# Batch 0's attention in pairs of chunks, W2 in contiguous rows, fewer filler matmuls, and a new order

## The chip, the core and the metric

The kernel runs on one core of one Trainium2 chip. The metric is the time of one execution on the device in microseconds (us). Three executions of the kernel before took 186.71, 187.40 and 190.95 us; the median, 187.4, stands for it. The engines are PE (matrix multiply; PEld is its loading of the stationary operand, which can run ahead), DVE and ACT (both read and write SBUF and the PSUM banks where matmuls put their results), POOL (SBUF alone), and SP, which here only issues DMAs. Each runs its own list of instructions in order and waits for the others at semaphores.

## The reference

Two parts in a row, for 4 batches, 8 heads of 48 columns (384 together) and 768 tokens. First a linear attention with a decaying state, for each batch and head:

```
for t in range(S):
    cur = einsum('bhd,bhe->bhde', u * k[t], v[t])
    y[t] = einsum('bhd,bhde->bhe', r[t], state + cur)
    state = w[t][..., None] * state + einsum('bhd,bhe->bhde', k[t], v[t])
```

Then, on x = y with the heads side by side (768 x 384 for each batch), a Fourier mix and a two-layer block:

```
mixed = real(fft(fft(x, axis=1), axis=2))
u  = x + mixed
un = (u - mean(u)) / sqrt(var(u) + 1e-6)
out = u + maximum(un @ w_ch1, 0) @ w_ch2      # 384 x 1536 and 1536 x 384
```

## The kernel before

**Attention.** `attention(b, c)` handles one chunk of 128 tokens, one token per partition, six chunks for each batch. It loads w, k, r and v of the chunk (`load_one`: for every token eight runs of 48 floats, 192 bytes), takes the logarithm of w on ACT, and sums it along the tokens by matmuls with triangular masks (L724, L728). Exponentials (L730, L743) turn the sums into factors; r and k are multiplied by them (L762, L519), transposed on PE (L778, L784) and copied out of PSUM (L542, L543). The scores (L794) are eight matmuls of 48 rows, for two heads side by side in the upper and the lower half of the array. They are masked on DVE (L799) and multiplied with v (L844); the state of the earlier chunks is added (L841). A chunk's own contribution to the state is summed on PE (L820, in batch 0 together with the old state through L817) and scaled on DVE (L828). The bonus term of u is computed without PE: r times k times u, summed over 48 columns (L751), times v (`vtd`, on POOL), added while y is taken from PSUM (L850).

**Mix and block.** `mix(b)` multiplies folded x by cosine and sine tables (L905 to L908), copies the result out and mirrors it (`hcs`, `hcr`), multiplies by the second set of tables (L931), adds x (`uf`, L933), takes mean and variance (L937, L939), transposes (L954, in batches 2 and 3 by a DMA) and runs the two layers in halves of 384 tokens: twelve groups of three matmuls with W1 (L978), a ReLU on ACT or DVE (L983, L985), then twelve matmuls with W2 for each 128 tokens (L996), and the output (L1000, DMA at L1004). The folding of x (`fold`, POOL or DVE) must have come for all six chunks before a batch's first mixing product is complete.

**Order.** All work is written as operations with numbers; `ORDER` names for every engine the sequence of these numbers, by hand of an earlier search, and the program waits only where an operation reads or overwrites what another engine makes. PSUM banks are given out in the same replay of the lists. SP issues all loads and outputs in the order of its list, POOL asks for the two weight matrices (`weights`, L702), each with a wait for one load of the inputs (`W_AFTER`). Input buffers are `NIN` = 7 for each of w, k, r and v.

**Filler.** While the tables of sines are made, PE runs 26 matmuls on a table (L1017), and `NW` = 32 more (L1053), whose results nobody reads, stand in its list among batch 0's attention.

Of the kernel before, what the change touches and what calls it, by code (L numbers as in the profile page):

```python
# [24 lines left out]
PAIR = 4  # L25
# [5 lines left out]
NW = 32  # L31
# [28 lines left out]
    "act": (  # L60
# [13 lines left out]
    "dve": (  # L74
# [323 lines left out]
def bass_rwkv6_finch__then__fnet_fourier_mix_kernel(  # L398
# [309 lines left out]
    def attention(b, c):  # L708
# [17 lines left out]
        if n >= 2:  # L726
            o.deps.add(masked[n - 2])
# [300 lines left out]
    for b in range(B):  # L1028
        if LATE_V and b == 0:
            for c in range(NC):  # L1030
                load(b, c)
# [55 lines left out]
```

## Time and profile before

| | |
|---|---|
| median of the three executions | 187.4 us |
| span of the profiled execution, first to last instruction | 184.6 us |
| PE busy | 175.4 us, 1718 matmuls |
| DVE, ACT, POOL busy | 154.4, 126.6, 103.6 us |
| moved by DMA | 28.99 MB in 116486 packets |
| first matmul with W1 (L978) | at 45.4 us |
| last matmul | ends near 182 us |

The profile comes from one execution, whose time lies beside the three above; its span leaves out what happens before the first and after the last instruction. Matmuls overlap in the array: one of 384 columns is shown with 326 ns, but the next starts 163 ns later, so busy time of PE is the union of such pieces. A line such as L519 is that of a helper through which many operations go; the names beside it (`rk`, `vtd`, `xf`) tell which one.

### The profile page before, as it was taken

The page shows a single profiled execution, that of the slowest core. Times are in us where ns is not written, and L with a number is a line of the kernel's source. Part 1 is how long each engine was busy: PE and PEld are TensorE (multiplying, and loading weights), DVE is VectorE, ACT ScalarE, POOL GpSimd, SP SyncE. Part 2 cuts the span into 40 slices and gives each one's busy share as a digit, 9 for nine tenths or more (in the row PEclk, how much of TensorE's full clock was granted, in tenths as well). Part 3 has the DMA queues.
Part 4 walks back from the last instruction along what each step waited for, and adds up shares of the span by engine and source line. Part 5 has one row for each costly group of instructions (what it writes and reads, how often), then busy time and mean ns, then how long its engine had stood idle before and what let it go on. Part 6 is the DMA issues. An engine that isn't in the chain of part 4 may idle for free.

```text
span 184.6 us, 4537 instructions
## 1 busy us (share of the span) xinstructions
PE 175.4 (95%) x1718; PEld 114.0 (62%) x1718; DVE 154.4 (84%) x360; ACT 126.6 (69%) x297; POOL 103.6 (56%) x125
## 2 busy tenths in 40 slices
PE   4988997988999999999999999999999999999994
PEld 2555654665566667767667766766666765665663
DVE  8779997999978999999998979999988878771134
ACT  4879696486885999798989897973852653125410
POOL 4038997775416967199899994999287100000000
DMA  6999998999999989999999997974780024330033
GB/s 122 205 203 196 183 208 159 196 187 187 184 190 188 201 168 242 204 219 209 186 250 185 212 216 117 220 140 107 170 181 0 4 85 97 74 109 22 0 128 128
DMA packets 116486, 28.99 MB, mean 157 GB/s; under 512 B 111345, under 2 KB 116082, under 8 KB 116466
## 3 DMA queue, kind: packets, MB, share of 16 engines
q1 hardware_dynamic: 114514, 26.36, 69.8%
q0 software_dynamic: 1952, 2.36, 7.7%
q8 instruction: 13, 0.21, 0.5%
q14 instruction: 7, 0.06, 0.1%
HBM read 23.59 MB, written 4.72 MB: 153 GB/s over the span
## 4 chain that ended last, share of the span: by engine, by line
PE 80%; POOL 7%; DVE 6%; DMA 2%; SPq 2%; issue 1%; ACT 1%; POOLq 0%; DVEq 0%; ACTq 0%
PE bank L996 26%; PE bank L978 26%; PE bank L931 6%; PE bank L908 3%; PE bank L1017 3%; PE bank L794 3%; DMA in_r<-in_r_dram 2%; SPq L563 2%; POOL rk L519 2%; PE bank L844 2%; PE bank L724 2%; PE bank L841 1%; PE bank L728 1%; POOL vtd L519 1%; PE bank L820 1%
## 5 line engine op out<-in xcount | busy, mean ns | idle before, releaser
L996 PE MATMUL bank<-w,ht 128*128 128x384 bf16 (+2 forms) x300 | 53.7, 320 | 0.0
L978 PE MATMUL bank<-unt,w 128*128 128x384 bf16 x288 | 53.3, 326 | 0.2 <-DVE unt L543 0.2
L985 ACT ACTIVATE ht<-bank 128x384 bf16<-128x384 f32 x78 | 35.6, 494 | 25.3 <-PE bank L978 25.0
L996 PEld LDWEIGHTS bank<-w,ht 128*128 128x128 bf16 x300 | 27.5, 98 | 15.8 <-issue 0.2
L978 PEld LDWEIGHTS bank<-unt,w 128*128 128x128 bf16 x288 | 26.8, 97 | 16.3 <-ACT unt L542 0.3
L799 DVE TENSOR_TENSOR ah<-bank,msk 128x512 bf16<-128x512 f32 x48 | 31.4, 680 | 3.3 <-PE bank L794 3.1
L519 POOL TENSOR_TENSOR vtd<-in_v,dc 128x384 f32<-128x384 f32 x24 | 20.7, 863 | 12.1 <-DVE dc L751 10.8
L519 POOL TENSOR_TENSOR rk<-rk,ub 128x384 f32<-128x384 f32 x22 | 22.9, 1042 | 6.9 <-DVE rk L519 6.7
L519 POOL TENSOR_TENSOR rkh<-in_k,e 128x384 bf16<-128x384 f32 x18 | 18.2, 1008 | 12.1 <-ACT e L743 12.0
L1000 DVE SCALAR_TENSOR_TENSOR osb<-bank,rstd,uf 128x384 f32<-128x384 f32 (+2 forms) x25 | 14.8, 594 | 11.8 <-PE bank L996 11.5
L519 POOL TENSOR_TENSOR rk<-in_r,in_k 128x384 f32<-128x384 f32 x18 | 18.0, 1000 | 4.3 <-DMA in_r<-in_r_dram 4.3
L542 ACT ACTIVATE rkt<-bank 128x512 bf16<-128x512 bf16 x29 | 16.9, 603 | 0.5 <-PE bank L778 0.2
L743 ACT ACTIVATE e<-bank 128x392 f32<-128x392 f32 (+1 forms) x24 | 11.7, 496 | 5.3 <-PE bank L737 3.0
L850 DVE TENSOR_TENSOR x<-bank,vtd 128x384 f32<-128x384 f32 x24 | 13.1, 551 | 2.3 <-PE bank L844 2.3
L730 ACT ACTIVATE bank<-bank 128x384 f32<-128x384 f32 x24 | 11.4, 479 | 4.4 <-PE bank L724 4.3
L533 ACT ACTIVATE un<-uf,agg 128x384 bf16<-128x384 f32 x18 | 10.6, 615 | 4.7 <-DVE agg L939 4.5
L933 DVE TENSOR_TENSOR uf<-bank,x 128x384 f32<-128x384 f32 x24 | 12.5, 546 | 1.4 <-PE bank L931 1.3
L762 DVE TENSOR_TENSOR rkh<-bank,in_r 128x384 bf16<-128x384 f32 x24 | 13.1, 548 | 0.7 <-ACT bank L730 0.6
L751 DVE TENSOR_REDUCE dc<-rk 128x8 f32<-128x384 f32 x24 | 12.9, 540 | 0.0
L937 DVE BATCH_NORM_STATS2 bst<-uf 128x6 f32<-128x384 f32 x24 | 12.7, 548 | 0.1
L533 ACT ACTIVATE vb<-in_v 128x384 bf16<-128x384 f32 x22 | 11.2, 520 | 1.8 <-DMA in_v<-in_v_dram 1.7
L533 ACT ACTIVATE lb<-in_w 128x384 bf16<-128x384 f32 x24 | 11.9, 520 | 0.6 <-DMA in_w<-in_w_dram 0.4
(128 smaller groups left out, 332.2 us busy)
## 6 DMA issues: line engine op xcount, KB each, us to landing
in_r<-in_r_dram SPq DMA_DIRECT2D x24, 192.0 KB, 3.9
in_k<-in_k_dram SPq DMA_DIRECT2D x24, 192.0 KB, 3.9
in_w<-in_w_dram SPq DMA_DIRECT2D x24, 192.0 KB, 3.9
in_v<-in_v_dram SPq DMA_DIRECT2D x24, 192.0 KB, 4.0
out_dram<-osb SPq DMA_DIRECT2D x23, 192.0 KB, 2.3
w<-in_moe_w_ch_dram POOLq DMA_DIRECT2D x2, 1152.0 KB, 13.4
out_dram<-osb SPq DMA_DIRECT2D x1, 128.0 KB, 1.8
rkt<-rkh SPq DMA_TRANSPOSE x6, 3.3
```

The costliest lines, as they stand in the source:

```text
L519: return lambda e: e.tensor_tensor(out=o, in0=a, in1=b, op=f)
L533: return lambda e: e.activation(o, a, f, **kw)
L542: {"act": lambda e: e.activation(o(), i(), ACTF.Copy), "dve": lambda e: e.tensor_copy(out=o(), in_=i())}, **kw)
L751: op("dve", v_1(DM), lambda e: e.tensor_reduce(out=dc[:, :], in_=rku[:, :, :], axis=mybir.AxisListType.X, op=ALU.add), r=[("RK", i2)], w=[ ...
L762: op("dve", v_1(DM), lambda e: e.tensor_tensor(out=rh[:, :, 0:D], in0=ps(tce)[:, 0:DM].rearrange("t (h d) -> t h d", d=D), in1=rt[:, :, :] ...
L799: masked[n] = op("dve", v_1(512), lambda e, x=x: e.tensor_tensor(out=ah[:, x:H:2, :], in0=ps(ta[x])[:, :].rearrange("p (h t) -> p h t", t= ...
L850: op("dve", v_1(DM), lambda e: e.tensor_tensor(out=xb[:, c, 0:DM], in0=ps(ty)[:, 0:DM], in1=vtd[:, :, :].rearrange("t h d -> t (h d)"), op ...
L937: op("dve", v_1(DM), lambda e, kb=kb, bs=bs: e.bn_stats(bs[:, :], uf[:, kb, :]), r=[("UF", i, kb)], w=[("BST", n % 4)])
L978: ins = e.matmul(ps(t)[:, 0:384], W1[:, m, 128 * j:128 * j + 128], unt[:, :, m, :], start=(m == 0), stop=(m == NM - 1))
L985: "act": lambda e, j=j, t=t, ht=ht: e.activation(ht[:, j, :], ps(t)[:, 0:384], ACTF.Relu, scale=-1.0)},
L996: ins = e.matmul(ps(t)[:, 0:hi - lo], ht[:, j, 128 * x:128 * x + 128], W2[:, j, lo:hi], start=(j == 0), stop=(j == NJ - 1))
L1000: op("dve", v_1(hi - lo) + 64, lambda e, kb=kb, t=t, o=o, lo=lo, hi=hi: e.scalar_tensor_tensor(out=o[:, lo:hi], in0=ps(t)[:, 0:hi - lo], s ...
```

## The change

Batch 0 is processed by a new function, `attention2`, in three pairs of chunks. A pair is loaded as 256 tokens, two neighbouring tokens on each partition: one DMA for each of w, k, r and v (`load_two`) with runs of 96 floats, 384 bytes. The even and the odd tokens (x = 0, 1) are kept as two operands of 128. The first chunk of the pair is then partitions 0 to 63, the second 64 to 127 (a = 0, 1):

- The cumulative sums need both operands: seven matmuls of 384 columns for a pair in place of four, with masks that stop at the half (`MSB`, `NLB`).
- The scores of a pair are 32 matmuls with 48 rows and 64 columns of output in place of 16 with 128; the masking instructions are as many and as large as before, with their own masks (`MSP`).
- The state and y sum over even and odd tokens, each matmul on 64 rows: twice as many of them. The bonus term, now kept in bf16, goes into y by two further matmuls with selection masks (`SEL`), so that the copy of y out of PSUM is a plain copy, on ACT or DVE.
- Transposed r is copied out with the even and odd tokens woven together again, so that its columns are in the order of the tokens.
- The masks are made in `halves`: an iota on POOL and twelve short operations on POOL and DVE at the start.

W2 is loaded with twelve contiguous rows on each partition instead of rows 128 apart; hidden unit 12p + j is then at partition p, so W1's columns for group j are taken 12 apart. `NW` falls from 32 to 8. The five lists of `ORDER` are new throughout. Batches 1 to 3 keep `attention`, and the scores, which went through a generator for an option that was off, are an operation of it. In the new POOL list eleven operations (three folds of batch 0 first) stand between the requests for W1 and for W2; in the old one W2 follows W1 directly. In the new SP list the last outputs are those of chunks 5 (in two pieces), 4 and 3 of batch 3; in the old one the two pieces of chunk 5 come last.

```diff
-PAIR = 4
+PAIRED = (0, 2, 4)
...
-NW = 32
+NW = 8
...
+    INA = {n: sb("in_%s" % n, [NIN, H * D], FP32) for n in "wkrv"}
+    INB = {n: [INA[n][:, i, :].rearrange("p (h d) -> p h d", d=D) for i in range(NIN)] for n in "wkrv"}
...
+    def load_two(c, n):
+        i = c % NIN
+        o = op("sp", 750, lambda e: e.dma_start(
+            INA[n][:, i:i + 2, :].rearrange("p x (h d) -> p (x h) d", h=H // 2),
+            src[n][0, :, c * CH:(c + 2) * CH, :].rearrange("h (t x) d -> t h (x d)", x=2)),
+               w=[("in", n, i), ("in", n, i + 1)], sem="in_%s%d" % (n, i), xfer=1423)
+        loads[0, c, n] = loads[0, c + 1, n] = o
...
+    def halves():
+        op("pool", 160, lambda e: e.iota(CJ[:, :], [[1, CH + 1]], base=-1, channel_multiplier=-2,
+                                         allow_small_or_imprecise_dtypes=True), w=["CJ"])
+        op("dve", 70, ts(TH[:, :], TC[:, 0:1], 63.5, -float(CH), ALU.is_gt, ALU.mult), r=["TC"], w=["TH"])
+        for i in range(2):
+            x = CJ[:, 1 - i:1 - i + CH]
+            either(140, 370, ts(MSP[i][:, :], x, TH[:, :], None, ALU.is_gt), r=["CJ", "TH"], w=[("MSP", i)])
+            either(140, 370, ts(SEL[i][:, :], x, TH[:, :], None, ALU.is_equal), r=["CJ", "TH"], w=[("SEL", i)])
...
-                          w=[n], sem=n, xfer=f)
+        for n, T, x, d, f in (("W1", W1, moe_w_ch1.rearrange("(q p) n -> p q n", p=128), 940, 8000),
+                              ("W2", W2, moe_w_ch2.rearrange("(p q) n -> p q n", p=128), 940, 7000)):
+            asked[n] = op("pool", d, lambda e, T=T, x=x: e.dma_start(T[:, :, :], x), w=[n], sem=n, xfer=f)
...
+    def attention2(c):
...
+        op("act", a_sb(2 * DM), act(L2[:, :, :, 0:D], wt, ACTF.Ln), r=win + ["LOGEXP"], w=lbs)
...
+        o = op("pe", mm(DM, 3), cums(t1, ((MSB[:, :], 0), (IDB[:, :], 0), (MSB[:, :], 1))), r=["MSB", "IDB"] + lbs, w=[t1])
+        op("pe", mm(DM, 2), cums(t0, ((MSB[:, :], 0), (MSB[:, :], 1))), r=["MSB"] + lbs, w=[t0])
+        op("pe", mm(DM, 2), cums(t2, ((NLB[:, :], 0), (NLB[:, :], 1))), r=["NLB"] + lbs, w=[t2])
...
+            def amat(e, x=x, ta=ta):
+                for q in range(HP):
+                    for a in range(2):
+                        for y in range(2):
+                            ins = e.matmul(ps(ta[y])[64 * a:64 * a + 64, 128 * q:128 * q + 128],
+                                           kT[x][64 * y:64 * y + D, q, 64 * a:64 * a + 64], rT[a][64 * y:64 * y + D, q, :])
+                return ins
+            op("pe", 450, amat, r=[("KTB", st4[x]), ("RTB", st4[0]), ("RTB", st4[1])], w=ta, tiled=True)
...
+                    for h in range(HP):
+                        for x in range(2):
+                            ins = e.matmul(ps(tds)[:, 96 * h:96 * h + 96], kflat[x][lo, 128 * h:128 * h + 128],
+                                           vb[x][lo, 2 * h:2 * h + 2, :].rearrange("t h d -> t (h d)"),
+                                           start=fst and x == 0, stop=(x == 1), skip_group_check=True)
...
+            def ymat(e, a=a, fst=fst, lo=lo, ty=ty, s_in=s_in):
+                for x in range(2):
+                    e.matmul(ps(ty)[:, 0:DM], SEL[x][lo, :], vtd[x][lo, :, :].rearrange("t h d -> t (h d)"), start=(x == 0), stop=False,
+                             skip_group_check=True)
+                for q in range(HP):
+                    if not fst:
+                        e.matmul(ps(ty)[:, 96 * q:96 * q + 96], rT[a][:, q, :], s_in[:, q, :], start=False, stop=False,
+                                 skip_group_check=True)
+                    for h in (2 * q, 2 * q + 1):
+                        for x in range(2):
+                            ins = e.matmul(ps(ty)[:, D * h:D * h + D], ah[x][lo, h, :], vb[x][lo, h, :], start=False, stop=(x == 1),
+                                           skip_group_check=True)
+                return ins
...
+            evict(lambda ca=ca: xb[:, ca, 0:DM], lambda ty=ty: ps(ty)[:, 0:DM], DM, r=[ty], w=[("X", 0, ca)])
+            fold(0, ca)
...
-                        ins = e.matmul(ps(t)[:, 0:384], W1[:, m, 128 * j:128 * j + 128], unt[:, :, m, :],
+                        ins = e.matmul(ps(t)[:, 0:384], W1[:, m, j:HID:NJ], unt[:, :, m, :],
...
-        step = 2 if b >= PAIR else 1
...
+        for c in range(NC):
+            if b == 0 and c in PAIRED:
+                attention2(c)
+            elif b or c - 1 not in PAIRED:
+                attention(b, c)
```

More of the change, by code (lines that the diff above doesn't have):

```diff
@@ L431, in bass_rwkv6_finch__then__fnet_fourier_mix_kernel @@
     NT = 4 if DMA_T < B * NC else 3
-    INB = {n: [sb("in_%s%d" % (n, i), [H, D], FP32) for i in range(NIN)] for n in "wkrv"}
+    INA = {n: sb("in_%s" % n, [NIN, H * D], FP32) for n in "wkrv"}
+    INB = {n: [INA[n][:, i, :].rearrange("p (h d) -> p h d", d=D) for i in range(NIN)] for n in "wkrv"}
     UB = sb("ub", [H, D], FP32)
-    LB = [sb("lb%d" % i, [H, 64], BF16) for i in range(NB)]
-    E2 = [sb("e2_%d" % i, [DM + H], FP32) for i in range(NB)]
+    LBA = sb("lb", [NB, H, 64], BF16)
+    LB = [LBA[:, i, :, :] for i in range(NB)]
+    E2 = [sb("e2_%d" % i, [DM + 2 * H], FP32) for i in range(NB)]
     RKH = [sb("rkh%d" % i, [2, H, 64], BF16) for i in range(NT)]
@@ L473, in bass_rwkv6_finch__then__fnet_fourier_mix_kernel @@
     ONE = sb("one", [2], BF16)
+    TH = sb("th", [1], FP32)
+    ONE4 = sb("one4", [2, 2], BF16)
+    CJ = SD[:, 0, 1, 0:CH + 1]
+    MSB, NLB, *MSP = (SD[:, 0, 0, 64 * i:64 * i + 64].bitcast(BF16) for i in range(6))
+    MSP, SEL = MSP[0:2], MSP[2:4]
+    HALVES = ["CJ", "MSB0", "NLB0", "MSB", "NLB"] + [(x, i) for x in ("MSP", "SEL") for i in range(2)]
     ONF = VTD[3].rearrange("p a b -> p (a b)")[:, 0:128]
@@ L551, in load @@
     def load(b, c):
+        if b == 0 and c in PAIRED:
+            for n in "wkrv":
+                load_two(c, n)
+                if c == 0 and n == "w":
+                    op("sp", 60, lambda e: e.dma_start(UR[0:1, :], u.rearrange("(o h) d -> o (h d)", o=1)), w=["UR"],
+                       sem="ur", xfer=300)
+                    bonus()
+            return
         for n in "wkr" + ("" if (b, c) in LATE_V else "v"):
@@ L585, in masks @@
         dset(384, ts(IDW[:, :], CI[:, :], 0.0, None, ALU.is_equal), r=["CI"], w=["IDB"])
+        if PAIRED:
+            halves()
         op("dve", 70, ts(PB[:, :, 0], TC[:, 0:1].to_broadcast([128, HP]), 63.5, -200.0, ALU.is_gt, ALU.mult),
@@ L589, in masks @@
            r=["TC"], w=["PB"])
+    def halves():
[6 more added lines that the diff above has]
+            either(140, 370, ts(SEL[i][:, :], x, TH[:, :], None, ALU.is_equal), r=["CJ", "TH"], w=[("SEL", i)])
+        either(140, 370, ts(MSB[:, :], CI[:, 128:256], 0.0, None, ALU.is_gt), r=["CI"], w=["MSB0"])
+        either(140, 370, ts(NLB[:, :], CI[:, 128:256], 0.0, -1.0, ALU.is_ge, ALU.mult), r=["CI"], w=["NLB0"])
+        either(50, 100, fill(MSB[0:64, 64:128], 0.0), r=["MSB0"], w=["MSB"])
+        either(50, 100, fill(NLB[0:64, 64:128], 0.0), r=["NLB0"], w=["NLB"])
+        either(50, 100, fill(ONE4[:, :, :], 0.0), w=["ONE4z"])
+        for a in range(2):
+            op("dve", 50, fill(ONE4[64 * a:64 * a + 64, a, :], 1.0), port=("dve",), r=["ONE4z"], w=[("ONE4", a)])
     def bonus():
@@ L700, in weights @@
     def weights():
-        for n, T, x, d, f in (("W1", W1, moe_w_ch1, 940, 8000), ("W2", W2, moe_w_ch2, 1070, 8000)):
-            asked[n] = op("pool", d, lambda e, T=T, x=x: e.dma_start(T[:, :, :], x.rearrange("(q p) n -> p q n", p=128)),
-                          w=[n], sem=n, xfer=f)
+        for n, T, x, d, f in (("W1", W1, moe_w_ch1.rearrange("(q p) n -> p q n", p=128), 940, 8000),
+                              ("W2", W2, moe_w_ch2.rearrange("(p q) n -> p q n", p=128), 940, 7000)):
+            asked[n] = op("pool", d, lambda e, T=T, x=x: e.dma_start(T[:, :, :], x), w=[n], sem=n, xfer=f)
@@ L874, in fold @@
         both = [("X", i, p), ("X", i, c)]
-        vec(DM, tt(sd[:, 0, 0:DM + 1], xb[:, p, 0:DM + 1], xb[:, c, 0:DM + 1], ALU.add), r=both, w=[("SD", z, 0)])
-        vec(DM, tt(sd[:, 1, 0:DM + 1], xb[:, p, 0:DM + 1], xb[:, c, 0:DM + 1], ALU.subtract), r=both, w=[("SD", z, 1)])
+        vec(DM, tt(sd[:, 0, 0:DM + 1], xb[:, p, 0:DM + 1], xb[:, c, 0:DM + 1], ALU.add), r=both, w=[("SD", z, 0)] + HALVES)
+        vec(DM, tt(sd[:, 1, 0:DM + 1], xb[:, p, 0:DM + 1], xb[:, c, 0:DM + 1], ALU.subtract), r=both, w=[("SD", z, 1)] + HALVES)
         have = [("SD", z, 0), ("SD", z, 1)]
@@ L1028, in bass_rwkv6_finch__then__fnet_fourier_mix_kernel @@
     for b in range(B):
-        if LATE_V and b == 0:
-            for c in range(NC):
-                load(b, c)
-        step = 2 if b >= PAIR else 1
-        for c in range(0, NC, step):
-            chunks = [attention(b, c + x) for x in range(step)]
-            parts = [next(x) for x in chunks]
-            def scores(e, parts=parts):
-                for f, _, _ in parts:
-                    ins = f(e)
-                return ins
-            op("pe", 207 * step, scores, r=sum([x[1] for x in parts], []), w=sum([x[2] for x in parts], []), tiled=True)
-            for x in chunks:
-                next(x, None)
-            if b * NC + c + 1 == LOG_FIRST:
-                sines()
-                mirrors()
-                tables_end()
+        for c in range(NC):
+            if b == 0 and c in PAIRED:
+                attention2(c)
+            elif b or c - 1 not in PAIRED:
+                attention(b, c)
         if b == 0:
```

117 lines of the change are left out of this document (115 added, 2 removed), and 122 rows, old and new, of the table ORDER.

## The prediction

> **What bounds the kernel now.** I read the stretches of the span first, cut where the matmul engine changes its kind of work: up to 8.7 us tables and early filler, to 45.4 us batch 0's attention and its mixing, then W1 and W2 matmuls of all batches with the later attention between, to 182.1 us. Columns: stretch, length, then busy time and instructions of PE, weight loads, DVE, ACT, POOL, then granted clock, DMA share and GB/s.
>
> ```profile
> 8.70:45.40 36.70, 32.63 (x393) 20.77 (x393) 32.99 (x74) 28.34 (x61) 27.48 (x32) 1.00 1.01 191
> 45.40:182.10 136.70, 136.58 (x1300) 90.10 (x1300) 113.76 (x243) 92.68 (x227) 74.25 (x79) 1.00 0.72 148
> ```
>
> The second stretch is a PE bound: 136.58 of 136.7 us busy. The first (the **front**) is not: PE is idle for 4.1 us, and part of its busy time is filler. The same view for the filler's line alone (columns end with clock, DMA and rate), and the chain of waits for what one matmul costs in a stream (start, length, engine, line, count):
>
> ```profile
> 8.70:45.40 36.70, 7.52 (x32) 2.66 (x32) 1.00 1.01 191
> ```
> ```profile
> 86.03 0.22 PE bank L784 x4
> 86.25 0.20 PE bank L844 x8
> 86.45 2.93 PE bank L978 x18
> ...
> 42.62 0.17 PE bank L820 x4
> ...
> 42.95 0.33 PE bank L794 x8
> ```
>
> A 384-column matmul takes 2.93/18 = 0.163 us of PE, a transpose 0.055, a 48-column one 0.025, a 96-column one 0.043, one of the scores (L794) 0.041. So the 32 fillers hold PE for 5.2 us, and the front's other 361 matmuls, each at its slot, for about 23 us: 51 of 384 or 386 columns 8.3, 38 of half that 3.1, 77 transposes 4.2, 56 scores 2.3, 48 of 96 columns 2.0, 48 of 48 columns 1.2, 40 small sums 1.0, the bonus broadcast 0.9. PE has 36.7 - 28 = 8 to 9 us to spare there, half of it hidden in the modelled ends of matmuls.
>
> What holds the front? The timeline about 31 us (bracket: idle before, and what ended it):
>
> ```profile
> 30.48 0.52 ACT L533 ACTIVATE vb<-in_v 128x384 bf16<-128x384 f32 x1 [1.31 <-DMA in_v<-in_v_dram]
> 30.60 0.83 POOL L519 TENSOR_TENSOR vtd<-in_v,dc 128x384 f32<-128x384 f32 x1 [1.06 <-DMA in_v<-in_v_dram]
> ...
> 31.55 0.40 PE L794 MATMUL bank<-rkt 48*128 48x128 bf16 x8 [1.12 <-ACT rkt L542]
> ...
> 31.99 0.69 DVE L799 TENSOR_TENSOR ah<-bank,msk 128x512 bf16<-128x512 f32 x1 [1.38 <-PE bank L794]
> ```
>
> All four engines stand because the values of chunk 4 land at 30.5 us; the DMA engines are full (1.01). But DVE is busy 33.0 of 36.7 us, so only about 1.4 us is lost there. The end of the front is a chain through DVE to the first W1 matmul; the weights come as late:
>
> ```profile
> 44.91 0.36 DVE L543 COPY unt<-bank 128x384 bf16<-128x384 bf16 x1
> ...
> 45.41 1.30 PE L978 MATMUL bank<-unt,w 128*128 128x384 bf16 x7 [0.15 <-DVE unt L543]
> ```
> ```profile
> 34.35 0.93 POOL L702 DMA_DIRECT2D w<-in_moe_w_ch_dram  x1
> 36.59 1.06 POOL L702 DMA_DIRECT2D w<-in_moe_w_ch_dram  x1 [1.31 <-DMA in_r<-in_r_dram]
> ```
> ```profile
> DMA to landing us min/median/max: 10.5/13.4/16.2
> ```
> ```profile
> 53.22 0.65 PE L996 MATMUL bank<-w,ht 128*128 128x384 bf16 x3
> ```
>
> W1 lands at 34.35 + 10.5 = 44.9, half a microsecond before it is read (the 16.2 would be too late for 45.41, so it is W2's); W2 at 36.6 + 16.2 = 52.8, 0.4 us before its first matmul.
>
> ```profile
> span 184.6 us, 4537 instructions
> ```
> ```profile
> 182.10 0.35 DVE L1000 SCALAR_TENSOR_TENSOR osb<-bank,rstd,uf 128x128 f32<-128x128 f32 x1 [0.19 <-PE bank L996]
> ```
>
> The profiled execution's span is 184.6 us, of which 2.5 follow the last matmul; 2.8 us lie around the span to the median of 187.4, and I count on the same 2.8 after.
>
> **The change part by part.** The end is (first W1 matmul) + (PE work left) + (tail), so I price each term.
>
> *Loads.* One packet's time comes from the DMA view of 5 to 15 us (only 192-byte runs) and that of 170 to 184.6 us (nearly only 1536-byte rows): packets, MB, share of 16 engines.
>
> ```profile
> q1 hardware_dynamic: 10809, 2.05, 105.0%
> ```
> ```profile
> q1 hardware_dynamic: 1008, 1.18, 23.4%
> ```
>
> That is 1.05 x 160/10809 = 15.5 ns at 190 bytes (16 engines for 10 us) and 0.234 x 233.6/1008 = 54 ns at 1170, so 0.039 ns a byte and 23 ns at 384. A load of two chunks has 1024 such packets, 64 for each DMA engine: 1.5 us, where two loads take 2.0 (ends: 1.0, if a packet costs the same; 2.0, if only bytes count). Twelve of them: 17.7 us for 23.8. In the new SP order v of chunks 4 and 5 is the 13th load of data: some 19 us of transfers with it, so it is in by 23 us and not at 30.5. The wait goes; what is late next is arithmetic. W2 in rows of 12 has one run per partition; at best it costs what W1's bytes cost, about 1 us of DMA less, used in the next term.
>
> *Extra matmuls*, three pairs: cumulative sums 9 x 0.163 = 1.5; the bonus now enters y through two selection matmuls, 12 x 0.163 = 2.0; y in halves 48 x 0.025 = 1.2; state in halves 20 x 0.043 = 0.9; scores in quarter tiles, 96 for 48. The last has no row: if four run abreast it costs nothing more, one after another as transposes do 96 x 0.055 - 2.0 = 3.3; I take L794's 0.041: 2.0. Sum 7.5 us (5.5 to 8.9). Removed: 24 fillers, 3.9. [...] No row here has a column tile.
>
> *DVE, ACT, POOL.* The y add leaves DVE (L850) for a plain eviction, five of six on ACT:
>
> ```profile
> L850 DVE TENSOR_TENSOR x<-bank,vtd 128x384 f32<-128x384 f32 x24 | 13.1, 551 | 2.3 <-PE bank L844 2.3
> L542 ACT ACTIVATE st<-bank 128x384 bf16<-128x384 f32 x12 | 5.8, 486 | 0.0
> ```
>
> DVE loses 5 x 0.55 = 2.7 us, ACT gains 5 x 0.49 = 2.4 and has 8.4 idle. In the front DVE takes back about 2 us of batch 1's instructions that the new order puts ahead (two masks of 0.68, one r product, one copy). Nine of the 13 mask operations go to DVE beside the table work of the first 9 us; they hide behind the early filler, which ends at 8.7, and cost up to 1 us if they don't. With the 1.4 us stall gone DVE alone could bring W1 to 45.4 - 2.1 = 43.3.
>
> POOL before it asks for W1 does 5 k products, 6 r products, 6 vtd and 5 folds instead of 3, 7, 6 and 8, and two masks: as long, without the 1.06 us wait, but its second k product now waits for the second pair's exponentials. Its prices:
>
> ```profile
> L519 POOL TENSOR_TENSOR rk<-in_r,in_k 128x384 f32<-128x384 f32 x18 | 18.0, 1000 | 4.3 <-DMA in_r<-in_r_dram 4.3
> ...
> L519 POOL TENSOR_TENSOR xf<-x 128x192 bf16<-128x192 f32 x5 | 2.9, 594 | 0.0
> ```
>
> I put the request at 33.6 (from 32.5 to 35) and W1 at 33.6 + 10.5 = 44.1. Behind W1 three folds, two products, a vtd, two k products, two fills and a product stand ahead of W2 on POOL, 1.8 + 2 + 0.8 + 2 + 0.4 + 1 = 8 us where 1.3 us of wait stood: W2 is asked for at 42.5, and with W1's 10.5 lands at 53.0. The vtd among them waits for a DVE reduction ordered just before the first mixing result, so a late DVE is passed on to W2 and by it to PE, in order, behind the first L996.
>
> *PE's own bound.* 23.1 + 7.5 + 8 fillers 1.3 + 1.6 of batch 1's matmuls that move ahead of W1 (scores 0.33, y 0.2, two sums 0.33, two totals 0.3, eight transposes 0.44) is 33.5: without any gap W1 starts at 42.2; with the 4.2 us of gaps now hidden in busy time, at 46.4. I take **44.0**, between these, with POOL's 44.1 and DVE's 43.3 about it. Then the first W2 matmul, 8.9 us on in the new order (12 groups of 0.49, the rest attention), is at 52.9, with W2 just landed.
>
> *Sum.* PE work after the first W1 matmul: 136.7 - 1.6 = 135.1. End of PE 44.0 + 135.1 = 179.1. The tail grows: the last output was the split one, now it is a whole chunk.
>
> ```profile
> L1000 DVE SCALAR_TENSOR_TENSOR osb<-bank,rstd,uf 128x384 f32<-128x384 f32 x23 | 13.9, 609 | 11.3 <-PE bank L996 11.1
> ...
> L1000 DVE SCALAR_TENSOR_TENSOR osb<-bank,rstd,uf 128x128 f32<-128x128 f32 x1 | 0.4, 351 | 0.2 <-PE bank L996 0.2
> ```
> ```profile
> out_dram<-osb SPq DMA_DIRECT2D x5, 192.0 KB, 1.9
> ...
> out_dram<-osb SPq DMA_DIRECT2D x1, 64.0 KB, 1.6
> ```
>
> That adds 0.26 + 0.3, with a queue of two outputs close together 0.7: 2.5 becomes 3.2 us. Span 182.3, with 2.8 around it **185.1 us**, 2.3 less than the median.
>
> **W1 by stride.** With W2 in contiguous rows, W1's columns are taken 12 apart, 24 bytes, in all 288 weight loads of L978. Nothing in this trace strides a weight load. What contiguous ones cost, four against one:
>
> ```profile
> 31.88 0.10 PEld L734 LDWEIGHTS bank<-pb,idw 128*128 128x128 bf16 x1
> 31.89 0.18 PEld L737 LDWEIGHTS bank<-one,lb 128*128 128x128 bf16 x4
> ```
>
> (0.18 - 0.10)/3 = 27 ns apart, so a load has a sixfold margin under the 163 ns of the matmul that it hides behind. Ends: no cost; twelvefold by bytes stepped over, 324 ns and (324 - 163) x 288 = 46 us. I take none, being nearest to the only row. [...]
>
> **The rivals.**
> 1. *The front shrinks further* (chance 0.28). Scores four abreast and fewer gaps: extras 5.5, W1 near 42, W2 asked for earlier by as much. 185.1 - 2.5 = 182.6 (181 to 183.6). For it: PE idles 4.1 us now behind one late load. Against: DVE and POOL come out at 43.3 and 44.1.
> 2. *The gain is eaten* (0.20): PE's gaps stay as they are (W1 at 46.4), or W2, which now has eight microseconds of POOL work ahead of it, lands two or three microseconds after it is wanted. 185.1 + 2.4 = 187.5 (186.6 to 190). For it: W2's 16.2 us before, and every engine of the front near full.
> 3. *Slower: strided weight loads* (0.14). Place: L978, in the stretch that is PE's alone. Every nanosecond over 163 is paid 288 times, 0.29 us; at 190 ns, seven times the contiguous load and well short of the twelvefold end, 7.8 us: 193. It decides from 163 + 2300/288 = 171 ns on, six times the contiguous load. Against: a margin of six.
> 4. *The loads gain nothing* (0.04): at 2.0 us a pair the late v comes at about 29 us and the extra matmuls are pure cost: 185.1 + 4 = 189.
>
> **How the numbers follow.** Forecast 185.1, chance 0.34, own range 183.7 to 186.6. Two per cent (3.7 us) is about what a measurement of this kernel can tell: the three runs lie between 186.7 and 191.0. Faster than 183.7: rival 1 and a little of the forecast, 0.30. Slower than 191.1: rival 3 and the ends of 2 and 4, 0.18. Between them 0.52. Leaving out rival 3 and the lowest end, the range is 181.3 to 190.5.
>
> **What would show it.** Loads right: transfers of batch 0 over by 23 us and no engine waiting for a DMA near 30. Front right: first L978 at 43 to 45, less than 2 us of PE idle before it. W2: an idle PE ahead of the first L996 says rival 2. Strides: a run of L978 at 163 ns a matmul says none; 170 and more, rival 3. Extras: the PE line for the quarter scores at 0.3 to 0.7 us for 16. The tail: 3.2 us after the last matmul. I would be wrong above all if one late engine in the front holds the three others, since their orders are fixed.

## The result and the profile after

The changed kernel takes 199.0 us (median of four runs, 198.5 to 200.7), 1.065 times the kernel before (95% interval 1.056 to 1.073): 6.5% slower, where 185.1 us, 2.3 less than before, were forecast. Ratios, here and below, leave out executions more than 1.5% above the fastest of their kernel; the kernel before has such ones too, most of them at 195 to 200 us with a mean clock of 0.965 to 0.982. The page of the changed kernel gives the span and, in 40 slices of it, the clock that PE was granted:

```profile
span 197.2 us, 4772 instructions
...
PEclk9999955555999999999999999999999999999999
```

Five slices of the front ran at half clock. The view of stretches, cut where the clock changes and at the first W1 matmul (columns as in the prediction: stretch, length, busy time and instructions of PE, weight loads, DVE, ACT and POOL, then clock, DMA share, GB/s):

```profile
8.70:24.90 16.20, 14.72 (x223) 9.29 (x221) 13.96 (x35) 13.38 (x28) 12.18 (x16) 1.00 1.05 253
24.90:48.70 23.80, 23.80 (x212) 14.78 (x212) 12.74 (x25) 11.95 (x26) 12.51 (x18) 0.50 0.96 182
48.70:58.60 9.90, 9.85 (x119) 6.88 (x118) 8.44 (x21) 8.40 (x18) 6.68 (x10) 1.00 0.26 33
58.60:194.00 135.40, 134.24 (x1267) 100.67 (x1263) 116.51 (x248) 87.43 (x214) 69.63 (x75) 1.00 0.62 132
```

For 23.8 us PE was busy at 0.50. At full clock that work would take about 14 us. This is an estimate: the 16 groups of y in it (shown below) take 0.47 us each and 0.35 at full clock, and the rest is halved, as matmuls of 386 columns are (0.32 us apart from 46.14 us on, 0.16 from 49.08 on). So the low clock costs some 10 us. DVE, ACT and POOL were busy for only half of that stretch: they waited for PE, directly or through one another (between 8.7 and 58.6 us ACT waited 4.3 us and DVE 3.3 for matmuls of L889, and POOL 6.2 for ACT's copies of y). From the first W1 matmul on nothing is lost: 135.4 us to the end of PE's work, where the prediction had 135.1. The whole miss lies ahead of the first W1 matmul.

What PE did as the clock fell and as it came back, in the timeline of the changed kernel (start, length, engine, line, tiles, stationary rows and columns, shape, count):

```profile
21.81 0.42 PE L844 MATMUL bank<-rkt 48*64 48x128 bf16 x16 [0.41 <-DVE ah L849]
22.16 0.49 PE L881 MATMUL bank<-vtd,sd 64*128 64x384 bf16 x2
22.59 0.22 PE L885 MATMUL bank<-st,rkt 128*128 128x96 bf16 x1
22.74 0.27 PE L889 MATMUL bank<-vb,ah 64*128 64x48 bf16 x4
22.94 0.22 PE L885 MATMUL bank<-st,rkt 128*128 128x96 bf16 x1
...
44.31 0.26 PE L885 MATMUL bank<-st,rkt 128*128 128x96 bf16 x1
44.51 0.34 PE L889 MATMUL bank<-vb,ah 64*128 64x48 bf16 x4
44.78 0.61 PE L975 MATMUL bank<-idw,rkh 128*128 128x128 bf16 x4
...
48.83 0.24 PE L1097 MATMUL bank<-cn,xf 128*128 128x193 bf16 x1
```

Each y of a pair's half, the first of all apart, changes four times from matmuls on 64 rows (L881, L889) to one on 128 rows (L885) and back. A group of one L885 and four L889 takes 22.94 - 22.59 = 0.35 us at full clock and 44.78 - 44.31 = 0.47 at half; in the kernel before, one full-row state matmul and two full-row ones take 0.093 by the prediction's slots (0.043 + 2 x 0.025). The clock fell 2.7 us after the first such y began, while the longest idle of PE here is 0.41 us, and it came back 4 us after the last of them had ended (44.78 to 48.8).

Other rows that answer to those of before. First W1 matmul; POOL's requests for W1 and W2, and their landing; the last outputs:

```profile
58.61 1.17 PE L1169 MATMUL bank<-unt,w 128*128 128x384 bf16 x6
```
```profile
41.22 1.00 POOL L741 DMA_DIRECT2D w<-in_moe_w_ch_dram  x1
...
56.98 0.61 POOL L741 DMA_DIRECT2D w<-in_moe_w_ch_dram  x1
```
```profile
DMA to landing us min/median/max: 9.0/9.2/9.4
```
```profile
193.52 1.27 DVE L1191 SCALAR_TENSOR_TENSOR osb<-bank,rstd,uf 128x384 f32<-128x384 f32 x2 [0.30 <-PE bank L1187]
```

### The profile page after: what moved, and what is told of

It reads as the page before. It is cut to its first block, busy times and chain, and to the rows that moved or that the text cites. A ratio compares the mean times of both kernels' runs of the same rounds, so it can differ in the third digit from the quotient of the medians.

```text
span 197.2 us, 4772 instructions
## 1 busy us (share of the span) xinstructions
PE 189.6 (96%) x1836; PEld 134.9 (68%) x1836; DVE 159.9 (81%) x372; ACT 127.1 (64%) x293; POOL 102.7 (52%) x127
## 4 chain that ended last, share of the span: by engine, by line
PE 78%; SPq 6%; DVE 6%; DMA 5%; ACT 2%; issue 1%; POOL 1%; DVEq 0%; POOLq 0%; ACTq 0%
PE bank L1169 21%; PE bank L1187 19%; SPq L583 6%; PE bank L1122 5%; PE bank L1099 4%; PE bank L1208 4%; PE bank L889 3%; DMA in_w<-in_w_dram 3%; PE bank L985 2%; DMA in_k<-in_k_dram 2%; PE bank L885 2%; PE bank L881 2%; PE bank L915 1%; PE bank L919 1%; PE bank L1035 1%; DVE ah L849 1%
## 5 line engine op out<-in xcount | busy, mean ns | idle before, releaser
L1176 ACT ACTIVATE ht<-bank 128x384 bf16<-128x384 f32 x69 | 32.2, 501 | 20.6 <-PE bank L1169 20.3
L1169 PEld LDWEIGHTS bank<-unt,w 128*128 128x128 bf16 x288 | 39.4, 144 | 6.0 <-issue 0.2
L523 POOL TENSOR_TENSOR vtd<-in_v,dc 128x384 f32<-128x384 f32 (+1 forms) x23 | 19.1, 835 | 12.4 <-DVE dc L942 9.9
L990 DVE TENSOR_TENSOR ah<-bank,msk 128x512 bf16<-128x512 f32 x36 | 22.8, 680 | 1.8 <-PE bank L985 1.7
L523 POOL TENSOR_TENSOR rk<-rk,ub 128x384 f32<-128x384 f32 x19 | 19.1, 1013 | 2.9 <-DVE rk L523 2.7
L537 ACT ACTIVATE un<-uf,agg 128x384 bf16<-128x384 f32 x21 | 12.7, 632 | 8.1 <-DVE agg L1130 8.1
L1174 DVE TENSOR_SCALAR ht<-bank 128x384 bf16<-128x384 f32 x27 | 14.0, 551 | 4.2 <-PE bank L1169 4.2
L523 POOL TENSOR_TENSOR xf<-sd 128x384 bf16<-128x384 f32 (+1 forms) x12 | 12.4, 1041 | 9.4 <-DVE sd L523 9.4
L1124 DVE TENSOR_TENSOR uf<-bank,x 128x384 f32<-128x384 f32 x24 | 12.7, 547 | 1.1 <-PE bank L1122 1.0
L537 ACT ACTIVATE lb<-in_w 128x384 bf16<-128x384 f32 (+1 forms) x21 | 11.8, 566 | 2.8 <-DMA in_w<-in_w_dram 1.5
L953 DVE TENSOR_TENSOR rkh<-bank,in_r 128x384 bf16<-128x384 f32 x18 | 9.9, 550 | 2.9 <-ACT bank L921 1.8
L1041 DVE TENSOR_TENSOR x<-bank,vtd 128x384 f32<-128x384 f32 x18 | 9.9, 548 | 0.5 <-PE bank L1035 0.3
## 6 DMA issues: line engine op xcount, KB each, us to landing
out_dram<-osb SPq DMA_DIRECT2D x23, 192.0 KB, 2.2
in_w<-in_w_dram SPq DMA_DIRECT2D x18, 192.0 KB, 4.0
in_r<-in_r_dram SPq DMA_DIRECT2D x18, 192.0 KB, 4.1
in_v<-in_v_dram SPq DMA_DIRECT2D x18, 192.0 KB, 4.0
in_k<-in_k_dram SPq DMA_DIRECT2D x18, 192.0 KB, 3.8
```

The costliest lines, as they stand in the source:

```text
L523: return lambda e: e.tensor_tensor(out=o, in0=a, in1=b, op=f)
L537: return lambda e: e.activation(o, a, f, **kw)
L990: masked[n] = op("dve", v_1(512), lambda e, x=x: e.tensor_tensor(out=ah[:, x:H:2, :], in0=ps(ta[x])[:, :].rearrange("p (h t) -> p h t", t= ...
L1124: op("dve", v_1(DM), lambda e, kb=kb, t=t: e.tensor_tensor(out=uf[:, kb, :], in0=ps(t)[:, 0:DM], in1=xb[:, kb, 0:DM], op=ALU.add), r=[t, ( ...
L1169: ins = e.matmul(ps(t)[:, 0:384], W1[:, m, j:HID:NJ], unt[:, :, m, :], start=(m == 0), stop=(m == NM - 1))
L1174: {"dve": lambda e, j=j, t=t, ht=ht: e.tensor_scalar(out=ht[:, j, :], in0=ps(t)[:, 0:384], scalar1=-1.0, scalar2=0.0, op0=ALU.mult, op1=AL ...
```

## The experiments

Three theories stood at first. **C**: the 24 removed fillers let the clock fall. **S**: the strided weight loads cost the time. **P**: the pairs' row and column tiled matmuls pull the clock down, whatever stands between them.

### Fillers back in the changed kernel

```
-NW = 8
+NW = 32
 # 24 more in PE's order: ahead of scores, transposes, y and state of 16 to 30 us
```

> The changed kernel with 24 more warming matmuls in batch 0's attention, 32 in all as before the change. Theory C (the removed warming matmuls let the granted clock fall to half from 25 to 47.5 us, 22.5 us at half speed, some 11 us lost): granted clock 1.00 throughout, first W1 matmul at 47 to 49 us instead of 58.7, span 185 to 188, time 188 to 191, within 2% of the kernel before. Theory S (the strided weight loads cost the time): no change, 198 to 200. Theory P (the row and column tiled matmuls of the pairs pull the clock down whatever stands between them): clock again at 0.50 for some 20 us, 198 to 201.

Measured: 196.1 us (median of six), ratio 1.052 (1.048 to 1.055). The profiled execution, the shortest with 193.0 us, had clock 1.00 all through; the others had a mean clock of 0.965 to 0.982. So with 32 fillers the clock held in one execution of six and fell less in the other five than in the changed kernel (0.939 to 0.948); but even with the clock full the first W1 matmul was late:

```profile
22.28 0.50 PE L883 MATMUL bank<-vtd,sd 64*128 64x384 bf16 x2
22.71 0.22 PE L887 MATMUL bank<-st,rkt 128*128 128x96 bf16 x1
22.86 0.27 PE L891 MATMUL bank<-vb,ah 64*128 64x48 bf16 x4
23.06 0.22 PE L887 MATMUL bank<-st,rkt 128*128 128x96 bf16 x1
...
52.59 1.17 PE L1171 MATMUL bank<-unt,w 128*128 128x384 bf16 x6
```

That is the timeline of this run: again 0.35 us for a group (22.71 to 23.06), and W1 at 52.6, not at 47 to 49. PE had become the bound of the front: it was busy for all of the seven stretches of 2 us from 18 to 32 us (2.00 in each). Theory C explains the clock at best in part, and none of the rest. Theory P's 20 us at half, whatever the fillers, didn't come either: 0.965 is about 14 us (2 x 0.035 x 197), an estimate that takes the whole shortfall as time at half; for the changed kernel's 0.939 it gives 24.1, where 23.8 were measured.

### Fillers out of the kernel before

```
-NW = 32
+NW = 8
 # indices 1446 to 1469 struck from PE's order, nothing else
```

> The kernel before with its last 24 warming matmuls taken out (8 left), all else as it was. Theory C: the granted clock falls to half somewhere between 15 and 35 us, time 193 to 200. Theory P and theory S: clock stays 1.00, time 186 to 190, or a little less than before, since 3.9 us of matmuls are gone.

Measured: 186.3 us, ratio 0.996 (0.992 to 1.000). One dip of the clock, in the view of stretches of this run:

```profile
8.70:20.50 11.80, 9.81 (x110) 5.83 (x107) 9.83 (x22) 9.65 (x22) 6.84 (x7) 1.00 0.98 192
20.50:24.20 3.70, 3.46 (x42) 3.08 (x42) 3.34 (x8) 2.36 (x6) 3.70 (x6) 0.56 1.05 208
24.20:45.20 21.00, 17.87 (x226) 11.55 (x222) 20.58 (x46) 16.04 (x35) 18.83 (x23) 1.00 1.08 198
```

It lasted under 4 us and cost nothing: the first W1 matmul came at 45.25, against 45.41. Theory C falls: taking the fillers away is not enough to lose the time, since in this kernel the clock is back at 24.2 us with the 24 gone. It can still be needed beside something else.

### The old loads of W1 and W2 in the changed kernel, and the new ones in the kernel before

```
-("W2", W2, moe_w_ch2.rearrange("(p q) n -> p q n", p=128), 940, 7000)
+("W2", W2, moe_w_ch2.rearrange("(q p) n -> p q n", p=128), 940, 7000)
-W1[:, m, j:HID:NJ]
+W1[:, m, 128 * j:128 * j + 128]
```

and the reverse of it in the kernel before.

> The changed kernel with W2 again loaded in 12 separated rows per partition and W1's columns again taken as 128 neighbours: the weight loads of the W1 line are contiguous. Theory C: weight loads fall from 144 to about 97 ns on the profile's line, but the time stays at 197 to 200, since the W1 matmuls stream at the same spacing as before. Theory S: 193 or less (at least 20 ns on each of 288 loads, 6 us).

> The kernel before with only W2 loaded in contiguous rows and W1's columns taken 12 apart. Theory C: 186 to 190, no difference, clock 1.00, W1 matmuls 0.163 us apart in a stream. Theory S: 193 or more, spacing 180 ns and over.

Measured: the changed kernel with the old loads 197.3 us, ratio 1.056 (1.051 to 1.062), with a half-clock stretch again (0.65 from 24 to 26 us and 0.50 from 26 to 32, mean clock 0.937 to 0.945 in the four executions); the kernel before with the new loads 187.2 us, ratio 1.004 (1.000 to 1.008). The line of W1's matmuls and its weight loads (nanoseconds min/median/max), in the changed kernel and, below, with the old loads:

```profile
L1169 PEld LDWEIGHTS bank<-unt,w x288: 138/143/168, 58.6 to 188.6; 128*128 128x128 bf16 x144
L1169 PE MATMUL bank<-unt,w x288: 323/326/383, 58.6 to 188.7; 128*128 128x384 bf16 x144
```
```profile
L1169 PEld LDWEIGHTS bank<-unt,w x288: 95/98/99, 58.4 to 187.1; 128*128 128x128 bf16 x144
L1169 PE MATMUL bank<-unt,w x288: 322/326/337, 58.5 to 187.3; 128*128 128x384 bf16 x144
```

A strided weight load is 45 ns longer in the middle and still lies beside its matmul, whose median stays at 326 ns. Only a few are late (383 against 337 at most); over the 245 spacings of neighbours in the trace, what lies above 163 ns adds up to 0.5 us (0.03 with the old loads). Theory S falls: that half microsecond comes after the first W1 matmul, and is no part of the 13 by which it is late.

### The y of a pair in another order

What the first run left over pointed to the changes of rows in y. Theory **G**: these changes leave the array standing; that is PE time, and it lets the clock fall. Theory **R**: 64 of 128 rows count as little activity in any order. Theory **W**: PE's waits for ACT and DVE do it. Two kernels part them, neither with an added filler: y grouped (four full-row matmuls first, then all half-row ones, so that the rows change once), and the old order with all of y and state on 128 rows.

```
+if not fst:
+    for q in range(HP):
+        e.matmul(ps(ty)[:, 96*q:96*q+96], rT[a][:, q, :], s_in[:, q, :], start=True, stop=False, ...)
 for x in range(2):
-    e.matmul(..., SEL[x][lo, :], ..., start=(x == 0), ...)
+    e.matmul(..., SEL[x][lo, :], ..., start=fst and x == 0, ...)
 for q in range(HP):
-    if not fst:
-        e.matmul(ps(ty)[:, 96*q:96*q+96], rT[a][:, q, :], s_in[:, q, :], start=False, ...)
     for h in (2 * q, 2 * q + 1): ...
```

> The changed kernel with the matmuls of a pair's y in another order: the four full-row ones on the state first, then the two selections and the 16 half-row ones, so that the array changes from half rows to full rows once for each y instead of four times. No filler is added. By the rows with 32 fillers a y of a later half costs 0.43 + 4 x 0.35 = 1.83 us and should cost some 1.15 so: five of them save 3.4 us at full clock. Theory G (the changes between half and full rows leave the array standing, and this standing time is what lets the clock fall): clock 1.00, first W1 matmul at 44 to 46 us, time 185 to 188. Theory R (matmuls on 64 of 128 rows count as little activity, however they are ordered): the clock falls again for some 15 to 20 us, first W1 at 51 to 56, time 192 to 197.

> The kernel with the grouped y and 12 more warming matmuls (20 in all), placed before scores and y of 17 to 26 us. Both theories: clock at least 0.98, first W1 at 46 to 49 us, time 186 to 190, between the grouped kernel at full clock and the same with 24 fillers. If the clock still falls, 12 fillers are too few and the time is 193 or more.

> The kernel with the grouped y and all 24 fillers back (32 in all). Clock 1.00. PE was busy without a gap from 12 to 52.6 us with these fillers, so the 3.4 us saved by grouping come off the end: first W1 at 49 to 50, time 189 to 191. If the row changes are not what y costs, as the run with fillers alone: 193 to 196.

In these three the flag `start` is set on each of the four state matmuls, and batch 0's y is not the reference's; the instructions and their sizes are all there.

```
-SEL[x][lo, :], vtd[x][lo, :, :] ...  ah[x][lo, h, :], vb[x][lo, h, :] ...  kflat[x][lo, ...], vb[x][lo, ...]
+SEL[x][:, :],  vtd[x][:, :, :]  ...  ah[x][:, h, :],  vb[x][:, h, :]  ...  kflat[x][:, ...],  vb[x][:, ...]
```

> The changed kernel in which selection, y and state matmuls of a pair run over all 128 rows instead of 64 (so each half also sums the other half's tokens: batch 0's y and state aren't those of the reference); as many matmuls, in the same order, no filler added. Theories G and R: no change of rows within a y, so it takes 0.33 + 4 x 0.15 = 0.9 us instead of 1.83, and the clock stays at 1.00: first W1 at 43 to 46, time 184 to 187. Theory W (the clock falls because PE waits for ACT and DVE between the scores from 20 to 22 us, with too few fillers, whatever the rows): the clock falls for some 4 to 15 us, first W1 at 47 or later, time 189 or more.

Measured: grouped 187.6 us, ratio 0.999 (0.994 to 1.003); with 12 fillers 187.9, 1.005 (1.000 to 1.009); with 24 fillers 191.0, 1.020 (1.013 to 1.026); on full rows 186.2, 0.993 (0.989 to 0.998). The clock is 1.00 in all four profiles (0.999 in the third); of the ten executions of the grouped kernel one, with 192.8 us, had a mean clock of 0.962. The old order on full rows, in the timeline of that run:

```profile
21.32 0.21 PE L885 MATMUL bank<-st,rkt 128*128 128x96 bf16 x1
21.37 0.26 PE L889 MATMUL bank<-vb,ah 128*128 128x48 bf16 x4
21.47 0.20 PE L885 MATMUL bank<-st,rkt 128*128 128x96 bf16 x1
```

On full rows a group takes 0.15 us (21.32 to 21.47) where it takes 0.35 on changing ones: as many matmuls, same order. So a change there and back costs some 0.2 us of PE. Grouped, the half-row matmuls stay, and the clock stays too: theory R falls, theory P with it, and so does W, since PE's waits ahead of the scores are still there (1.30 us of the 2 from 20 to 22 were busy in the grouped run, 1.26 in the changed kernel). Fillers now only cost: 191.0 us with 24 of them, against 187.6 with none added.

### The grouped y with the flag set once, and with the old loads

```
-    e.matmul(ps(ty)[:, 96*q:96*q+96], ..., start=True, stop=False, ...)
+    e.matmul(ps(ty)[:, 96*q:96*q+96], ..., start=(q == 0), stop=False, ...)
```

> The changed kernel with the grouped y, now with the flag that opens the bank set on the first of the four state matmuls alone, so that nothing is left out; the same instructions in the same order as the first grouped kernel. Theory G (the changes between half and full rows in y are the whole loss): clock 1.00, first W1 matmul at 46 to 47.5, time 185.5 to 188.5, 10 us or more below the changed kernel. If the first grouped kernel was fast only because it dropped something: 195 or more.

> The same with W2 loaded and W1's columns taken as before the change (contiguous weight loads). In the changed kernel's trace 238 spacings of W1 matmuls lie together 0.46 us over 163 ns, in the kernel with the old loads 0.03 us. So the stride should be worth about 0.5 us: 185 to 188, within half a per cent of the run beside it. If the stride costs as much as the two changed kernels differed, 1 to 1.7 us.

Measured: 186.3 us, ratio 0.998 (0.995 to 1.002): some 12.7 us less than the changed kernel, for the order of the 22 matmuls in each of five y's. One such y and the scores behind it, in the timeline of this run:

```profile
26.25 0.34 PE L882 MATMUL bank<-st,rkt 128*128 128x96 bf16 x4
26.52 0.49 PE L885 MATMUL bank<-vtd,sd 64*128 64x384 bf16 x2
26.86 0.56 PE L890 MATMUL bank<-vb,ah 64*128 64x48 bf16 x16
27.35 0.42 PE L844 MATMUL bank<-rkt 48*64 48x128 bf16 x16
```

It takes 1.10 us, where two selections and four groups took 0.43 + 4 x 0.35 = 1.83. The clock is 0.997 or more in all twelve executions, where the four of the changed kernel had 0.939 to 0.948. So the order of y is the loss, in PE's time and in the clock, as theory G has it. How the changes reach the clock is not shown; that the array's standing counts as idleness is an argument only.

With the old loads the kernel takes 188.3 us, ratio 1.006 (1.002 to 1.009), so the new loads are worth about 0.7%, against the sign that I expected of the stride. The first W2 matmuls, with the new loads and with the old ones:

```profile
54.23 1.47 PE L1188 MATMUL bank<-w,ht 128*128 128x384 bf16 x8
```
```profile
56.15 1.14 PE L1188 MATMUL bank<-w,ht 128*128 128x384 bf16 x6 [1.67 <-DMA w<-in_moe_w_ch_dram]
```

The bracket of the last row is PE's wait for W2: in twelve separate rows W2, asked for at 44.0 us, takes 12.0 to land and comes 1.7 us too late in this front; in one contiguous row per partition, asked for at 43.9, it takes 9.5 and is there in time. W1's stride, half a microsecond, is the price of it.

### Halves in the kernel before

```
 for h in (2 * q, 2 * q + 1):
-    ins = e.matmul(..., ah[:, h, :], vb[:, h, :], start=first, stop=True, ...)
+    for lo in (0, 64) if b == 0 else (None,):
+        p = slice(0, 64) if b == 0 else slice(0, 128)
+        ins = e.matmul(..., ah[p, h, :], vb[p, h, :], start=first and not lo, stop=lo != 0, ...)
```

> The kernel before without 24 fillers (which alone cost nothing), and in batch 0 each of y's 128-row matmuls replaced by two of 64 rows (both on the first 64 tokens, so the others are left out), between the full-row matmuls as they stand: twenty changes of rows more in the front. Theory G: as in the changed kernel one group of a state matmul and four halves takes 0.30 to 0.35 us at full clock instead of 0.096, and the clock falls to half until some 4 us after the last such y, for 10 to 20 us; time 190 to 198. Theory D (the changes cost only PE's time, and something else in the changed kernel pulls the clock): clock at 0.99 as without halves, time 186 to 190.

> The same halves in the kernel before with all its 32 fillers. Theory G: the fillers keep the clock at 1.00 and PE pays only the changes, 20 x 0.25 = 5 us, of which its 4 us of idle time in the front can hide a part: 187 to 192, below the kernel without fillers. If halves cost nothing here: 186 to 188.

Measured: with 8 fillers 193.5 us, ratio 1.031 (1.024 to 1.038); with all 32, clock 1.00, 190.7 us, ratio 1.020 (1.014 to 1.026). The timeline of the second, the first W1 matmul among it, and the view of stretches of the first:

```profile
22.11 0.22 PE L841 MATMUL bank<-st,rkt 128*128 128x96 bf16 x1
22.26 0.27 PE L846 MATMUL bank<-vb,ah 64*128 64x48 bf16 x4
22.46 0.22 PE L841 MATMUL bank<-st,rkt 128*128 128x96 bf16 x1
...
50.01 1.30 PE L980 MATMUL bank<-unt,w 128*128 128x384 bf16 x7 [0.15 <-DVE unt L543]
```
```profile
20.70:27.10 6.40, 6.40 (x64) 4.50 (x63) 4.74 (x10) 3.35 (x7) 4.24 (x6) 0.50 1.00 199
```

The price comes out in the other kernel as well: 0.35 us a group, 20 groups of 0.25 more, and W1 4.6 us later. So does the clock. The profiled execution, the shortest of the four, was at half for 6.4 us, against 3.7 without halves; the other three had mean clocks of 0.956 to 0.962, which is about 14 to 17 us at half (2 x 0.038 x 191 and 2 x 0.044 x 194), within the 10 to 20 I expected. Theory D of that expectation, that something else in the changed kernel pulls the clock, falls. And the fillers matter once there are changes: with all 32 the clock is 0.999 or 1.00 in all four executions. In this kernel only both together, changes of rows and few fillers, lose 6 us and more to half clock in every execution.

### Two changes to a y, and no fillers in the attention

```
 # two changes: state matmuls of q and q + 1 ahead of eight halves, twice
+if not fst and q % 2 == 0:
+    for z in (q, q + 1):
+        e.matmul(ps(ty)[:, 96*z:96*z+96], rT[a][:, z, :], s_in[:, z, :], start=False, ...)
```

> The changed kernel with two changes to full rows in each later y instead of four or one: two state matmuls, eight halves, two state matmuls, eight halves, after the selections. If PE pays by the change and the clock falls only when changes lie densely: a y of some 1.45 us, and either clock 1.00, first W1 matmul at 47 to 49 and 187 to 190, or a shorter fall of the clock (4 to 12 us), first W1 at 50 to 55 and 191 to 195. If any change within a y lets the clock fall as four do: first W1 at 55 or later, 195 or more. By the account that only four to a y do it: as the grouped kernel, 186 to 188.

> The kernel with the grouped y and none of the warming matmuls among batch 0's attention (8 removed). If the grouped front keeps the clock by its own work: clock at least 0.99, time 184.5 to 187.5, at most 1.3 us below the grouped kernel, and the fillers were needed for nothing. If it is at the edge: clock 0.95 to 0.98 and 189 to 195.

Measured: two changes 193.2 us, ratio 1.031 (1.021 to 1.041). Three executions lie between 192.0 and 193.9 us with a mean clock of 0.964, which is about 13.7 us at half (2 x 0.036 x 190). The profiled one had 0.938 and 195.7 us; its first such y, and the stretch at half, which began 1.2 us later:

```profile
20.71 0.50 PE L881 MATMUL bank<-vtd,sd 64*128 64x384 bf16 x2
```
```profile
21.90:45.80 23.90, 23.90 (x238) 14.98 (x239) 13.74 (x27) 12.83 (x28) 14.04 (x20) 0.50 1.01 193
```

That is as long as in the changed kernel; all four fell for longer than the 4 to 12 us that I expected. The grouped kernel with none of the 8 fillers: 187.2 us (median of four, too scattered for an interval). Three executions lie between 185.2 and 188.3 us with a clock of 0.999 or 1.00; the fourth had 0.964 and 190.9. So the clock goes with the changes: about 20 to 24 us at half in each execution of the changed kernel (four to a y), 14 to 24 with two, and with one almost none (clock 0.997 or more) in 21 of the 22 executions of the two grouped kernels with the new loads and 8 fillers. That grouping holds it without these fillers is not shown, with one execution of four against it.

## Why the prediction was wrong

**The step that failed** is PE's own bound of the front: the term "y in halves 48 x 0.025", and the clock of 1.00, which the sum took over from before while it removed 24 fillers at 3.9 us of PE time and nothing else. No rival had it otherwise. The changed y costs 0.2 us at each change of rows and its way back; and with 8 fillers these changes let the clock fall for 23.8 us. The y of the front was priced at 5.3 us in all (2.1 in the kernel before, 2.0 for the selections, 1.2 for the halves); by the slots between the starts of its matmuls it takes 9.8 at full clock in the run with 32 fillers, and 6.2 grouped. The grouped kernel, with the clock full, has its first W1 matmul at 45.4 and the changed kernel at 58.6: 13.2 us. Of these, 9.8 - 6.2 = 3.6 are the changes at full clock; the other 9.6 are the clock's, near the 10 estimated above.

The price of a change could have been read in the trace of before, where the scores, on 48 rows, stand among full-row matmuls:

```profile
67.20 0.40 PE L794 MATMUL bank<-rkt 48*128 48x128 bf16 x8
67.53 0.66 PE L978 MATMUL bank<-unt,w 128*128 128x384 bf16 x3
...
97.98 0.81 PE L996 MATMUL bank<-w,ht 128*128 128x384 bf16 x4
98.73 0.62 PE L794 MATMUL bank<-rkt 48*128 48x128 bf16 x16
99.28 0.82 PE L996 MATMUL bank<-w,ht 128*128 128x384 bf16 x4
```

The four matmuls of L996 take 0.75 us to the start of the scores (97.98 to 98.73), where four slots of 0.163 are 0.65: 0.10 for the way in. Eight scores take 0.33 us (67.20 to 67.53) and sixteen 0.55 (98.73 to 99.28), so eight alone are 0.22, and 0.11 is the way out. Together that is the 0.2 us. The prediction divided 0.33 by 8 and took the 0.041 for the slot of a score. That many changes let the clock fall, no row of before showed.

The other steps, in the prediction's order:

- **Loads: right.** Between 5 and 15 us, the DMA view of the changed kernel (packets, MB, share of 16 engines):

```profile
q1 hardware_dynamic: 7836, 2.97, 109.1%
```

1.091 x 160/7836 = 22.3 ns a packet, 23 forecast. The values of the last pair were asked for at 15.0 us and in at most 5.4 us later, ahead of the 23 forecast. In the grouped kernel no engine waits for a DMA ahead of the first W1 matmul; the stall at 30 us is gone. Rival 4 is out.
- **Extra matmuls.** Scores were over-priced, the rest under-priced: 16 quarter scores 0.35 us (21.81 to 22.16), 22 ns each and not 41; six times 0.35 is 2.1, so about 0.1 us more than before and not 2.0. A half of y in a block takes 0.031 us, not 0.025 (16 in 27.35 - 26.86 = 0.49), a half of the state 0.055, not 0.043 (eight in 0.44). In the grouped kernel these nearly cancel, in the changed one the changes of rows add 3.6.
- **POOL: nearly right** where the clock held. In the grouped kernel W1 is asked for at 33.3 us (33.6 forecast) and W2 at 43.9 (42.5). W1 takes 11.8 us to land, not 10.5, and is there at 45.1 (44.1 forecast), just ahead of its first matmul; in the changed one both were late behind PE, 41.2 and 57.0, and still in time.
- **DVE: off by 2.6 us.** The grouped kernel's front, in the view of stretches:

```profile
8.70:45.40 36.70, 34.94 (x544) 24.53 (x542) 34.85 (x80) 32.89 (x71) 31.06 (x41) 1.00 1.00 214
```

DVE is busy for 34.9 us where it was 33.0 in the same stretch before, though I had it lose 0.7: 1.7 us of work on tables and masks (L527) no longer hides before 8.7 us, and the rest is spread over small pieces. PE is busy for 34.9 us too. So the front ends at 45.4 as before, and not at 44.0, with DVE, PE and W1's landing all close to that time; which of them holds it, no run parts. That is where most of the expected gain of 2.3 us went, apart from the clock.
- **After the first W1 matmul: right.** 135.4 us for 135.1; tail 197.2 - 194.0 = 3.2, as forecast. The 2.8 us around the span are 198.95 - 197.2 = 1.8: the prediction had set the median of three executions against the span of one. So the grouped kernel's 186.3, near the 185.1, is in part luck: its front is 1.4 us longer than forecast, and this term 1.0 shorter.
- **The strides: right** in the sum. The median spacing of W1's matmuls stays 163 ns; rival 3's 7.8 us measured 0.5. The loads themselves take 143 ns for 98; these 45 ns lie beside the matmul, whose median is 326 ns with either.
- **Rival 2's mechanism exists**: W2 after it is wanted, 1.7 us, but only with the old rows of W2. Rival 1 didn't come: W1 didn't go below 45.1 in any run.

## What to carry to other kernels

Keep matmuls on the same rows together: each change from half rows to full rows and back costs some 0.2 us of PE here, and a group that slots of 43 and 25 ns put at 0.14 us took 0.35. Before thinning out filler matmuls, or splitting matmuls into smaller ones, price the clock as a term of its own: 24 us at half cost some 10 us here, more than any single term of this change. Reordering the matmuls within one accumulation cost nothing here and undid nearly all of the loss.

## What the runs showed that I had not expected

- The clock fell to half with PE recorded as busy 91% of the time (14.72 of 16.2 us) and no idle over 0.41 us. With the half-row matmuls of a y in a block the clock was 0.997 or more in 21 of 22 executions, with them interleaved 0.939 to 0.948. How many changes in what time it takes isn't settled: two to a y give 14 to 24 us at half, and the same halves in the kernel before 6 to 17, or none with 32 fillers.
- Once down it stayed down in the changed kernel for as long as such y's came, though PE had no recorded gap in 23.8 us; it was back at 48.7 us, after 4 us of full-row matmuls, most of them mixing. By the clock of the 2-us stretches in the profiles it stood at half ahead of W1 for 3.4 us in the kernel before without 24 fillers (0.74, 0.50 and 0.91 from 20 to 26 us) and for 6.8 in the same with halves (0.58, 0.50, 0.50 and 0.71 from 20 to 28); in the changed kernel and with two changes to a y it was 23.8 and 23.9: near one, two and seven times 3.4.
- The fillers of the kernel before cost nothing and brought nothing as long as its y stood on full rows (0.996, 0.992 to 1.000, without 24 of them). With halves in y they held the clock (0.999 or 1.00 with all 32, 0.956 to 0.982 with 8). In a front that PE bounds, 24 cost 3.4 us (191.0 against 187.6).
- No version beat the kernel before by 2%. The grouped one is level with it (0.998, 0.995 to 1.002).
